# Token-order loads and DMA transposes for q and k of the last batch

## The chip, the cores and the metric

The kernel runs on one core of a Trainium2 chip. The metric is the device time of one execution in microseconds (us), the median of several. The spans in the profiles are about 2 us shorter than the timed executions, because they run from the first to the last instruction. Each execution is listed with the mean granted clock of PE. PE is TensorE's matmuls, DVE VectorE, ACT ScalarE, POOL GpSimd, SP the engine whose queue issues most plain DMAs and all DMA transposes here.

## The reference, cut to what matters

Four batches of attention (8 heads, 768 positions, head size 64; each position sees 8 global and the 96 latest positions), then a mixing block over tokens and channels.

```python
scores = scale * np.matmul(q, k.transpose(0, 1, 3, 2))      # per batch and head
...                                                         # bias by distance, mask
a = np.exp(scores - scores.max(-1)); a = a / a.sum(-1)
x = np.matmul(a, v)                                         # heads side by side: 768 x 512

theta = x @ w_theta
zr, zi = x * np.cos(theta), x * np.sin(theta)
u = x + w_tok_r @ zr + w_tok_i @ zi                         # mixing over tokens, per batch
out = u + np.maximum(u @ w_ch, 0.0)
```

q, k and v are float32; the kernel casts them to bfloat16 while it loads them.

## The kernel before

PE needs q and k with the head dimension on the partitions: `qT` and `kT`, 128 x 768 for a pair of heads. The kernel before loads q and k so that a partition gets six successive tokens of a head (768 B written per row), casts the layout on DVE (`qkn`), transposes 128 x 128 blocks on PE into PSUM and copies them out, qT by DVE and kT by ACT. I call this the prep of a pair. `kG` is a copy of kT in which each block starts with the global positions.

```python
def load_qk(b, h0, n, which=(0, 1)):
    qk = loads[b][0]
    for i_ in which:
        nc.gpsimd.dma_start(
            out=qk[:, i_, h0:h0 + n].rearrange("p h t d -> p h (t d)"),
            in_=(q, k)[i_][b, h0:h0 + n].rearrange("h (p t) d -> p h (t d)", p=T))

def prep(b, p):
    ...                                                     # prep_copy: two DVE casts into qkn
    for i_, dst in ((0, qT), (1, kT)):
        ps = ps_small([T, NT, T], BF)
        with behind("pe"):
            for t_ in range(NT):
                nc.tensor.transpose(ps[:, t_, :], qkn[:, t_, i_].rearrange("p h d -> p (h d)"), ident)
        ...
        if i_ == 0:
            nc.vector.tensor_copy(out=dst, in_=src)
        else:
            nc.scalar.copy(out=dst, in_=src)
    qkT[(b, p)] = [qT, kT, None]
    kglob(b, p)                                             # two DVE copies: kG
```

The main loop runs over the batches. While batch b is mixed (`mix`, `chan`: long matmuls), the attention of batch b + 1 is woven into it by weights (`weave`; its last argument says at which part of the mixing the attention ends). The prep of batch b + 2 is woven in there too (`ahead`). So batch 3, the last, is prepared in the mixing of batch 1. Then comes theta of batch b + 1, which needs `xT`, the transpose of the attention's result; for batches 1 to 3 it is made by DMA, as `uT` is, the transpose of the mixing's result.

```python
def xtrans(b, p, copy=nc.vector.tensor_copy):
    if b:
        nc.sync.dma_start_transpose(
            out=xT_sb[b][:, p, :].rearrange("p (t s) -> p t s", t=NT),
            in_=x_sb[b][:, p].rearrange("p t d -> p (t d)"))
        return
...
ahead = [lambda p=p: prep(b + 2, p) for p in range(NP)] if b + 2 < B else []
order = th[:4] + rest[:2] + th[4:] + rest[2:] if b else []  # theta of b, last chan of b - 1
if b == 1:
    order.insert(0, lambda: load_behind(3, xT_sb[1][0:1, NC - 1, 0:1]))   # q, k, v of batch 3
...
weave(main, side, 0.3 if b == 0 else 0.0, 0.9)
```

A compile-time scheduler settles the order of each engine's and each queue's instructions; every queue then works in that order. `behind(e)` forces an instruction behind the last one that was marked as anchor `e`.

I call the time from the first theta matmul of one batch to that of the next a stage: stage 0 ends with theta of batch 1; stage 1 is theta and mixing of batch 1 with the attention of batch 2, and so on. A "boundary" is the stretch from the first theta matmul to the first score matmul of the next batch.

The softmax here doesn't subtract the row's maximum and nothing guards it: scores larger than these inputs give would overflow.

Of the kernel before, what the change touches and what calls it, by code (L numbers as in the profile page):

```python
# [10 lines left out]
BF = mybir.dt.bfloat16  # L11
# [5 lines left out]
def kernel(  # L17
# [13 lines left out]
    nc = tc.nc  # L31
    B, H, S, D = q.shape
    T = 128
    NT = S // T
    DM = H * D
    NC = DM // T
    NP = H // 2
    NG = int(n_global)
# [9 lines left out]
    att = ctx.enter_context(tc.tile_pool(name="att", bufs=2))  # L48
# [7 lines left out]
    def ps_small(shape, dtype):  # L56
        return small.tile(shape, dtype, name="ps", tag="ps")
# [3 lines left out]
    loads = {}  # L61

    def alloc_qk(b):
        loads[b] = [ld.tile([T, 2, H, NT, D], BF, name="qk"), None]

    def alloc_v(b):
        vn = loads[b][1] = ld.tile([T, H, NT, D + 1], BF, name="vn")
        nc.vector.memset(vn[:, :, :, D:D + 1], 1.0)  # L68
# [4 lines that stand above are left out]
            nc.gpsimd.dma_start(  # L73
                out=qk[:, i_, h0:h0 + n].rearrange("p h t d -> p h (t d)"),
                in_=(q, k)[i_][b, h0:h0 + n].rearrange("h (p t) d -> p h (t d)", p=T))

    def load_v(b, h0, n):
        vn = loads[b][1]
        nc.gpsimd.dma_start(out=vn[:, h0:h0 + n, :, 0:D].rearrange("p h t d -> p (h t) d"),  # L79
                            in_=v[b, h0:h0 + n].rearrange("h (t p) d -> p (h t) d", p=T))  # L80
# [8 lines left out]
    for i_, eng in ((1, nc.sync), (0, nc.scalar)):  # L89
        eng.dma_start(out=qk32[:, i_].rearrange("p h t d -> p h (t d)"),  # L90
                      in_=(q, k)[i_][0, 0:2].rearrange("h (p t) d -> p h (t d)", p=T))
# [5 lines left out]
    alloc_qk(0)  # L97
    alloc_v(0)
    load_qk(0, 2, 2)
    load_v(0, 0, 4)  # L100
    load_qk(0, 4, 2)
    load_qk(0, 6, 2)
    load_v(0, 4, 4)

# [64 lines left out]
    x_sb, xT_sb = {}, {}  # L169
    qkT = {}  # L170

    anchor = {}
# [5 lines left out]
    def behind(eng):  # L178

        return tc.issue_after(anchor[eng]) if eng in anchor else nullcontext()  # L180
# [24 lines left out]
    def kglob(b, p):  # L205
        kT = qkT[(b, p)][1]
        kG = qkT[(b, p)][2] = att.tile([T, NT - 2, T], BF, name="kG", bufs=6)
        nc.vector.tensor_copy(out=kG, in_=kT[:, T:(NT - 1) * T].rearrange("p (t n) -> p t n", t=NT - 2))  # L208
        nc.vector.tensor_copy(out=kG[:, :, 0:NG], in_=kT[:, None, 0:NG].to_broadcast([T, NT - 2, NG]))  # L209

    qkns = {}

    def prep_copy(b, p):
        qk = loads[b][0]
        qkn = qkns[b, p] = att.tile([T, NT, 2, 2, D], BF, name="qkn", bufs=2)
        with behind("dve"):
            for i_ in range(2):
                nc.vector.tensor_copy(  # L218
                    out=qkn[:, :, i_].rearrange("p t h d -> p h t d"), in_=qk[:, i_, 2 * p:2 * p + 2])

    def prep(b, p):
        if p == 0:
            prep_copy(b, 0)
        if p + 1 < NP:
            prep_copy(b, p + 1)
        qkn = qkns[b, p]
        qT = att.tile([T, S], BF, name="qT", bufs=6)
        kT = att.tile([T, S], BF, name="kT", bufs=6)
# [6 lines that stand above are left out]
            dst = dst.rearrange("p (n t) -> p n t", t=NT)  # L235
            src = ps.rearrange("p t n -> p n t")
# [4 lines that stand above are left out]

        qkT[(b, p)] = [qT, kT, None]
        kglob(b, p)

    ebuf = {}

# [51 lines left out]
    def scores(b, p, c):  # L298
        score_mms(b, p, c)
        score_exp(b, p, c)  # L300
# [41 lines left out]

    def xtrans(b, p, copy=nc.vector.tensor_copy):
        if b:
            nc.sync.dma_start_transpose(
                out=xT_sb[b][:, p, :].rearrange("p (t s) -> p t s", t=NT),
                in_=x_sb[b][:, p].rearrange("p t d -> p (t d)"))
            return
        ps = ps_small([T, S], BF)
        for st in range(NT):  # L350
            nc.tensor.transpose(ps[:, st * T:(st + 1) * T], x_sb[b][:, p, st, :], ident)
        copy(out=xT_sb[b][:, p, :], in_=ps)
# [44 lines left out]
    def utrans(b, tt):  # L397
        u = u_sb[b, tt]
        uT = moe.tile([T, NC, T], BF, name="uT", bufs=5)
        uTs[(b, tt)] = uT  # L400
        if b and (b, tt) != (B - 1, NT - 1):
            nc.sync.dma_start_transpose(out=uT, in_=u)
            return
        ps = ps_small([T, NC, T], BF)
        for dc in range(NC):
            nc.tensor.transpose(ps[:, dc, :], u[:, dc * T:(dc + 1) * T], ident)  # L406
        nc.scalar.copy(out=uT, in_=ps)  # L407
# [16 lines left out]
    def load_all_qk(b):  # L424
        alloc_qk(b)
        load_qk(b, 0, 8)

    def load_all_v(b):
        alloc_v(b)
        load_v(b, 0, 8)  # L430
# [4 lines left out]
    def load_behind(b, tile):  # L435
        g = nc.gpsimd.tensor_copy(out=gate, in_=tile).ins
        with tc.issue_after(g):
            load_all_qk(b)
            load_all_v(b)

    def attention_steps(b, preps):

        steps = []
        add = lambda w, f, *a: steps.append((w, lambda: f(*a)))
        add(0, alloc_x, b)
        chunks = [(p, c) for p in range(NP) for c in range(NT // 2)]
        ahead = [preps[:1], preps[1:2], preps[2:]] if preps else [[]] * 3
        for i_ in range(0, len(chunks), 2):
            steps.append((1800, lambda i_=i_: [scores(b, *pc) for pc in chunks[i_:i_ + 2]]))
            if i_ == 0:  # L450
                add(0, vglob, b, 0, H)
            if i_ == 8:
                steps.extend((1536, f) for f in ahead[0])
            for p in [p for p in range(NP) if (i_ // 2, p) in ((2, 0), (3, 1), (5, 2))]:
                add(1600, lambda p=p: [values(b, p, 0), values(b, p, 1)])
                add(800, xtrans, b, p)
        steps.extend((1536, f) for f in ahead[1])
        add(1600, lambda: [values(b, NP - 1, 0), values(b, NP - 1, 1)])
        add(800, xtrans, b, NP - 1)
        steps.extend((1536, f) for f in ahead[2])  # L460
        return steps
# [22 lines left out]
    dve, act = nc.vector.tensor_copy, nc.scalar.copy  # L484
# [24 lines left out]
    for p in range(NP):  # L509
# [29 lines left out]
        if p:  # L539
            xtrans(0, p - 1, act if p == NP - 1 else dve)  # L540
# [14 lines left out]
    for b in range(B):  # L555
        nxt = b + 1 if b + 1 < B else None
        lag = 3
        th = [lambda c=c, j=j: theta(b, c, j) for c in range(NT // 2) for j in range(2)]
        pre = [lambda p=p: prep(1, p) for p in range(NP)] if b == 0 else []
        ahead = [lambda p=p: prep(b + 2, p) for p in range(NP)] if b + 2 < B else []  # L560
        order = th[:4] + rest[:2] + th[4:] + rest[2:] if b else []
        if b == 1:
            order.insert(0, lambda: load_behind(3, xT_sb[1][0:1, NC - 1, 0:1]))
        for f in order:
            f()
        main = []
        for tt in range(NT):
            for g in range(NT // 2):
                if (b, tt) != (B - 1, NT - 1):
                    main.append((2048, lambda tt=tt, g=g: mix(b, tt, g)))  # L570
                if b == 0 and g == 1 and tt + 1 < NT:
                    main.append((1536, lambda tt=tt: trans_w(tt + 1)))
                if tt >= lag and g == 0 and (b, tt) != (B - 1, NT - 1):
                    main.append((2048, lambda tt=tt: chan(b, tt - lag)))
                if b == 0 and tt and g == 1:
                    main.append((512, lambda tt=tt: utrans(b, tt - 1)))
            if b and (b, tt) != (B - 1, NT - 1):
                main.append((0, lambda tt=tt: utrans(b, tt)))
        side = [(1536, f) for f in pre]
        if b == 0:  # L580
            side[:0] = [(0, lambda: load_all_v(2))]
        side += attention_steps(nxt, ahead) if nxt else []
        weave(main, side, 0.3 if b == 0 else 0.0, 0.9)
        rest = [lambda tt=tt, b=b: chan(b, tt) for tt in range(NT - lag, NT)]
        if b == 0:
            rest.insert(1, lambda b=b: utrans(b, NT - 1))
# [44 lines left out]
```

## Time and profile before

The time was 176.44 us, the median of three (176.27 to 177.23). The profiled execution has a span of 174.7 us at clock 1.000.

The first parts of the page give busy time and share of the span, then the busy tenths in 40 slices of 4.4 us (9 is 90% or more; DMA is the mean of 16 DMA engines).

```profile
PE 160.6 (92%) x1505; PEld 86.4 (49%) x1530; DVE 133.9 (77%) x300; ACT 102.2 (58%) x128; POOL 26.3 (15%) x31
...
DVE  7678965778999999996779999796866847723443
...
DMA  5999999999999972479999955133145371414335
```

PE is nearly always busy. DVE is full from slice 11 to 18 (stage 0) and again from slice 22 to 25 (the end of stage 1). The DMA engines are full until about 60 us, and once more around 80 to 100 us, when batch 3 is loaded.

The prep's groups (line, engine, operation, out<-in, shape, count, then total busy us and mean ns of one, then the idle time before them). Each group is for three batches; a third is batch 3's.

```profile
L238 DVE COPY qT<-ps 128x768 bf16<-128x768 bf16 x12 | 11.4, 947 | 0.0
L233 PE MATMUL ps<-ident,qkn 128*128 128x128 bf16 x144 | 10.7, 219 | 0.4 <-DVE qkn L218 0.3
L240 ACT COPY kT<-ps 128x768 bf16<-128x768 bf16 x12 | 9.6, 798 | 10.3 <-PE ps L233 10.3
L218 DVE COPY qkn<-qk 128x768 bf16<-128x768 bf16 x24 | 7.4, 342 | 0.0
```

The busy time overlaps for pipelined instructions. What a prep costs PE is read better from the chain that ended last (start, length, what), where batch 3's four preps stand:

```profile
94.93 0.67 PE ps L233 x12
...
100.46 0.67 PE ps L233 x12
...
104.39 0.67 PE ps L233 x12
...
105.95 0.87 PE ps L233 x12
```

Busy time by stretches (start:end, length, then PE, PEld (weight loads), DVE, ACT and POOL, then granted clock, DMA share and GB/s) for stage 1 and for stage 2, which has the same mixing and attention but no prep:

```profile
72.00:108.50 36.50, 35.79 (x347) 19.46 (x351) 32.68 (x72) 24.59 (x30) 4.77 (x4) 1.00 1.26 156
108.50:142.00 33.50, 32.91 (x294) 16.58 (x298) 25.23 (x47) 19.63 (x23) 0.00 (x0) 1.00 0.34 84
```

PE (the first engine) binds in both; stage 1 is 3 us longer. The theta lines of PE's timeline, with the idle time before them in brackets:

```profile
108.38 3.62 PE L368 MATMUL pb<-w_theta_bf,xT 128*128 128x512 bf16 x15
...
141.48 1.46 PE L368 MATMUL pb<-w_theta_bf,xT 128*128 128x512 bf16 x6
143.44 2.33 PE L368 MATMUL pb<-w_theta_bf,xT 128*128 128x512 bf16 x10 [0.50 <-DMA xT<-x_sb]
```

Theta of batch 2 (108.38) runs through.

### The profile page before, as it was taken

What the parts mean: (1) busy time and instruction counts of PE and PEld (TensorE: products, weight loads), DVE (VectorE), ACT (ScalarE), POOL (GpSimd) and SP (SyncE); (2) the same over time, 40 slices, a digit from 0 to 9 for tenths busy, and PEclk for the clock granted to TensorE, in tenths of its full rate; (3) what the DMA queues carried; (4) which work ended last, traced back from release to release, by engine and by line L of the source; (5) the groups of instructions that cost most, each with busy time, mean ns of one, the idle gap of its engine ahead of it and who ended that gap; (6) DMA issues with size and microseconds to landing.
All of it is one profiled execution on the core that took longest, in us unless ns stands there. A gap on an engine that the chain in (4) does not pass through costs nothing.

```text
span 174.7 us, 3707 instructions
## 1 busy us (share of the span) xinstructions
PE 160.6 (92%) x1505; PEld 86.4 (49%) x1530; DVE 133.9 (77%) x300; ACT 102.2 (58%) x128; POOL 26.3 (15%) x31
## 2 busy tenths in 40 slices
PE   6469878999999899999999999999999989999991
PEld 1245555456746566544455565443554634444440
DVE  7678965778999999996779999796866847723443
ACT  2479676999497694499854813779447408500010
POOL 8983355004000000190000000000000000000000
PEclk9999999999999999999999999999999999999999
DMA  5999999999999972479999955133145371414335
GB/s 157 183 192 182 206 208 208 204 205 165 166 204 167 159 116 45 109 90 216 244 148 103 168 135 135 34 121 90 21 87 134 90 168 27 172 31 101 114 90 180
DMA packets 58225, 24.36 MB, mean 139 GB/s; under 512 B 44256, under 2 KB 55264, under 8 KB 58208
## 3 DMA queue, kind: packets, MB, share of 16 engines
q0 software_dynamic: 35216, 12.45, 70.5%
q1 hardware_dynamic: 22576, 11.15, 28.8%
q10 hardware_dynamic: 416, 0.52, 0.9%
q8 instruction: 12, 0.20, 0.5%
q14 instruction: 5, 0.04, 0.1%
HBM read 25.69 MB, written 6.29 MB: 183 GB/s over the span
## 4 chain that ended last, share of the span: by engine, by line
PE 56%; DVE 23%; ACT 13%; DMA 4%; issue 2%; DVEq 0%; ACTq 0%
PE ps L388 25%; PE ps L413 10%; PE pb L368 7%; DVE x_sb L341 4%; PE pb L274 4%; PE pb L331 3%; ACT e L281 3%; PE ps L368 3%; ACT etab L133 3%; ACT cs L374 3%; DVE qT L238 2%; DVE e L291 2%; DMA qk<-in_k_dram 2%; DVE kG L208 2%; PE ps L233 2%
## 5 line engine op out<-in xcount | busy, mean ns | idle before, releaser
L388 PE MATMUL ps<-zri,w_tokT 128*128 128x512 bf16 x271 | 67.6, 379 | 1.2 <-issue 0.5
L281 ACT ACTIVATE e<-pb 128x1024 bf16<-128x1024 f32 (+1 forms) x48 | 43.5, 958 | 21.1 <-PE pb L274 21.0
L388 PEld LDWEIGHTS <-w_tokT 128*128 128x128 bf16 x288 | 25.9, 98 | 27.6 <-DVE w_tokT L160 0.6
L393 DVE TENSOR_TENSOR u<-x_sb,ps 128x512 bf16<-128x512 bf16 x24 | 16.4, 682 | 14.0 <-PE ps L388 14.0
L413 PE MATMUL ps<-w_ch_bf,uT 128*128 128x512 bf16 x94 | 23.7, 379 | 0.3 <-DVE u L393 0.2
L377 DVE TENSOR_TENSOR zri<-x_sb,cs 128x512 bf16<-128x512 bf16 x48 | 17.9, 418 | 7.9 <-ACT cs L374 7.6
L419 DVE SCALAR_TENSOR_TENSOR o_sb<-ps,u 128x512 f32<-128x512 f32 (+1 forms) x25 | 16.5, 662 | 3.1 <-PE ps L413 3.1
L274 PE MATMUL pb<-qT,kT 64*128 64x128 bf16 x224 | 15.6, 219 | 1.4 <-DVE qT L202 0.3
L291 DVE TENSOR_TENSOR e<-e,etab 128x1024 bf16<-128x1024 bf16 (+1 forms) x24 | 14.7, 616 | 2.5 <-ACT e L281 2.5
L274 PEld LDWEIGHTS <-kT 64*128 64x128 bf16 x224 | 9.1, 94 | 14.5 <-issue 12.5
L374 ACT ACTIVATE cs<-pb,halfpi 128x1024 bf16<-128x1024 f32 x8 | 8.9, 1115 | 11.5 <-PE pb L368 11.5
L240 ACT COPY kT<-ps 128x768 bf16<-128x768 bf16 x12 | 9.6, 798 | 10.3 <-PE ps L233 10.3
L368 PE MATMUL pb<-w_theta_bf,xT 128*128 128x512 bf16 x62 | 14.9, 379 | 0.6 <-DMA xT<-x_sb 0.5
L407 ACT COPY uT<-ps 128x512 bf16<-128x512 bf16 x7 | 4.1, 587 | 18.6 <-PE ps L406 18.6
L368 PEld LDWEIGHTS <-xT 128*128 128x128 bf16 x96 | 9.2, 98 | 11.1 <-DMA xT<-x_sb 1.0
L331 PEld LDWEIGHTS <-e 128*128 128x128 bf16 x352 | 12.6, 97 | 3.3 <-issue 1.6
L413 PEld LDWEIGHTS <-uT 128*128 128x128 bf16 x96 | 8.9, 98 | 10.0 <-ACT uT L407 0.3
L274 PE MATMUL pb<-qT,kG 64*128 64x128 bf16 x128 | 11.7, 217 | 1.5 <-DVE kG L209 1.4
L341 DVE TENSOR_TENSOR x_sb<-pb,rec 128x768 bf16<-128x768 f32 x12 | 11.4, 948 | 0.2
L79 POOL DMA_DIRECT2D vn<-in_v_dram x5 | 9.6, 1912 | 12.2 <-DVE vn L68 10.6
L238 DVE COPY qT<-ps 128x768 bf16<-128x768 bf16 x12 | 11.4, 947 | 0.0
L233 PEld LDWEIGHTS <-qkn 128*128 128x128 bf16 x144 | 9.0, 97 | 4.4 <-DVE qkn L218 1.4
(72 smaller groups left out, 200.9 us busy)
## 6 DMA issues: line engine op xcount, KB each, us to landing
out_dram<-o_sb SPq DMA_DIRECT2D x23, 256.0 KB, 2.2
qk<-in_q_dram POOLq DMA_DIRECT2D x3, 768.0 KB, 17.4
qk<-in_k_dram POOLq DMA_DIRECT2D x3, 768.0 KB, 19.3
vn<-in_v_dram POOLq DMA_DIRECT2D x3, 768.0 KB, 22.0
w_nat<-in_moe_w_tok_r_dram POOLq DMA_DIRECT2D x3, 384.0 KB, 14.0
w_nat<-in_moe_w_tok_i_dram POOLq DMA_DIRECT2D x3, 384.0 KB, 15.2
vn<-in_v_dram POOLq DMA_DIRECT2D x2, 384.0 KB, 8.8
qk<-in_q_dram POOLq DMA_DIRECT2D x3, 192.0 KB, 6.7
```

The lines of the kernel that those rows point to most:

```text
L238: nc.vector.tensor_copy(out=dst, in_=src)
L274: nc.tensor.matmul(pb[:, hh, o:o + T], lhsT=lhsT, rhs=qT[R, (own, nxt)[part]], start=bool(b), stop=bool(b) or (jt == NT - 1 or (j == 1 and ...
L281: ins = nc.scalar.activation(e_c, pb[:, :, 0:n], AF.Exp, scale=scale).ins
L291: nc.vector.tensor_mul(e_c, e_c, tab[:, :, s0:s0 + n // T].rearrange("p a s n -> p a (s n)"))
L331: nc.tensor.matmul(o, lhsT=l_, rhs=r_, start=(i_ == 0), stop=(i_ == len(mms) - 1))
L341: nc.vector.tensor_mul(xv, po4[:, :, :, 0:D], rec.to_broadcast([T, n, NT, D]))
L368: nc.tensor.matmul(pb[j_] if last else pb[:, j_, :], lhsT=xT[:, dc, st(j_)], rhs=w_theta_bf[:, dc, :], start=(dc == 0), stop=(dc == NC - 1))
L377: nc.vector.tensor_mul(zri[b][:, i_, 2 * c + j_, :].rearrange("p (g d) -> p g d", g=NP), xb[:, :, 2 * c + j_, :], cs[:, i_, j_].rearrange( ...
L388: anchor["pe"] = nc.tensor.matmul(ps, lhsT=w_tokT[wi][:, st, tt * T:(tt + 1) * T], rhs=zri[b][:, wi, st, :], start=(st == 0 and wi == 0), ...
L393: anchor["dve"] = nc.vector.tensor_add(u_sb[b, tt].rearrange("p (g d) -> p g d", g=NP), x_sb[b][:, :, tt, :], ps.rearrange("p (g d) -> p g ...
L413: nc.tensor.matmul(ps_c, lhsT=uT[:, dc, :], rhs=w_ch_bf[:, dc, :], start=(dc == 0), stop=(dc == NC - 1))
L419: nc.vector.scalar_tensor_tensor(o_sb[:, cols], in0=ps_c[:, cols], scalar=0.0, in1=u[:, cols], op0=ALU.max, op1=ALU.add)
```

## The change

Its intent: take the prep of the last batch off PE, DVE and ACT. q and k of batch 3 are loaded in token order (a partition is a token within a block of 128, both heads of a pair side by side), so that one DMA transpose makes a whole qT or kT. The first four heads are loaded in stage 0, behind the last casts of batch 1, the others at the start of stage 1. Pair 0 is transposed in the mixing of batch 1, pairs 1 to 3 at the boundary to batch 2. The kG copies are made when the attention of batch 3 begins.

```diff
--- before.py
+++ after.py
@@ -74,6 +74,15 @@
                 out=qk[:, i_, h0:h0 + n].rearrange("p h t d -> p h (t d)"),
                 in_=(q, k)[i_][b, h0:h0 + n].rearrange("h (p t) d -> p h (t d)", p=T))
 
+    def load_qk_tokens(b, h0, n):
+        qk = loads[b][0]
+        for h in range(h0, h0 + n):
+            for i_ in range(2):
+                pair = qk[:, i_, h // 2 * 2:h // 2 * 2 + 2].rearrange("p h t d -> p (h t d)")
+                nc.gpsimd.dma_start(
+                    out=pair.rearrange("p (t h d) -> p t h d", t=NT, h=2)[:, :, h % 2],
+                    in_=(q, k)[i_][b, h].rearrange("(t p) d -> p t d", p=T))
+
     def load_v(b, h0, n):
         vn = loads[b][1]
         nc.gpsimd.dma_start(out=vn[:, h0:h0 + n, :, 0:D].rearrange("p h t d -> p (h t) d"),
@@ -205,8 +214,10 @@
     def kglob(b, p):
         kT = qkT[(b, p)][1]
         kG = qkT[(b, p)][2] = att.tile([T, NT - 2, T], BF, name="kG", bufs=6)
-        nc.vector.tensor_copy(out=kG, in_=kT[:, T:(NT - 1) * T].rearrange("p (t n) -> p t n", t=NT - 2))
-        nc.vector.tensor_copy(out=kG[:, :, 0:NG], in_=kT[:, None, 0:NG].to_broadcast([T, NT - 2, NG]))
+        with behind("dve") if b == B - 1 else nullcontext():
+            nc.vector.tensor_copy(
+                out=kG, in_=kT[:, T:(NT - 1) * T].rearrange("p (t n) -> p t n", t=NT - 2))
+            nc.vector.tensor_copy(out=kG[:, :, 0:NG], in_=kT[:, None, 0:NG].to_broadcast([T, NT - 2, NG]))
 
     qkns = {}
 
@@ -241,6 +252,16 @@
 
         qkT[(b, p)] = [qT, kT, None]
         kglob(b, p)
+
+    def prep_dma(b, p):
+        qk = loads[b][0]
+        qkT[(b, p)] = [None, None, None]
+        for i_ in (1, 0):
+            to = qkT[(b, p)][i_] = att.tile([T, S], BF, name=("qT", "kT")[i_], bufs=6)
+            with behind("sp"):
+                nc.sync.dma_start_transpose(
+                    out=to.rearrange("p (t s) -> p t s", t=NT),
+                    in_=qk[:, i_, 2 * p:2 * p + 2].rearrange("p h t d -> p (h t d)"))
 
     ebuf = {}
 
@@ -342,9 +363,9 @@
 
     def xtrans(b, p, copy=nc.vector.tensor_copy):
         if b:
-            nc.sync.dma_start_transpose(
+            anchor["sp"] = nc.sync.dma_start_transpose(
                 out=xT_sb[b][:, p, :].rearrange("p (t s) -> p t s", t=NT),
-                in_=x_sb[b][:, p].rearrange("p t d -> p (t d)"))
+                in_=x_sb[b][:, p].rearrange("p t d -> p (t d)")).ins
             return
         ps = ps_small([T, S], BF)
         for st in range(NT):
@@ -399,7 +420,7 @@
         uT = moe.tile([T, NC, T], BF, name="uT", bufs=5)
         uTs[(b, tt)] = uT
         if b and (b, tt) != (B - 1, NT - 1):
-            nc.sync.dma_start_transpose(out=uT, in_=u)
+            anchor["sp"] = nc.sync.dma_start_transpose(out=uT, in_=u).ins
             return
         ps = ps_small([T, NC, T], BF)
         for dc in range(NC):
@@ -435,7 +456,7 @@
     def load_behind(b, tile):
         g = nc.gpsimd.tensor_copy(out=gate, in_=tile).ins
         with tc.issue_after(g):
-            load_all_qk(b)
+            load_qk_tokens(b, H // 2, H // 2)
             load_all_v(b)
 
     def attention_steps(b, preps):
@@ -445,10 +466,14 @@
         add(0, alloc_x, b)
         chunks = [(p, c) for p in range(NP) for c in range(NT // 2)]
         ahead = [preps[:1], preps[1:2], preps[2:]] if preps else [[]] * 3
+        if b == B - 1:
+            add(0, kglob, b, 0)
         for i_ in range(0, len(chunks), 2):
             steps.append((1800, lambda i_=i_: [scores(b, *pc) for pc in chunks[i_:i_ + 2]]))
             if i_ == 0:
                 add(0, vglob, b, 0, H)
+            if b == B - 1 and i_ in (0, 2, 6):
+                add(0, kglob, b, (1, 2, 0, 3)[i_ // 2])
             if i_ == 8:
                 steps.extend((1536, f) for f in ahead[0])
             for p in [p for p in range(NP) if (i_ // 2, p) in ((2, 0), (3, 1), (5, 2))]:
@@ -557,8 +582,11 @@
         lag = 3
         th = [lambda c=c, j=j: theta(b, c, j) for c in range(NT // 2) for j in range(2)]
         pre = [lambda p=p: prep(1, p) for p in range(NP)] if b == 0 else []
-        ahead = [lambda p=p: prep(b + 2, p) for p in range(NP)] if b + 2 < B else []
+        ahead = [[lambda p=p: prep(2, p) for p in range(NP)], [lambda p=p: prep_dma(3, p) for p in range(1)],
+                 [], []][b]
         order = th[:4] + rest[:2] + th[4:] + rest[2:] if b else []
+        if b == 2:
+            order[:0] = [lambda p=p: prep_dma(3, p) for p in range(1, NP)]
         if b == 1:
             order.insert(0, lambda: load_behind(3, xT_sb[1][0:1, NC - 1, 0:1]))
         for f in order:
@@ -579,6 +607,7 @@
         side = [(1536, f) for f in pre]
         if b == 0:
             side[:0] = [(0, lambda: load_all_v(2))]
+            side.append((0, lambda: (alloc_qk(3), load_qk_tokens(3, 0, H // 2))))
         side += attention_steps(nxt, ahead) if nxt else []
         weave(main, side, 0.3 if b == 0 else 0.0, 0.9)
         rest = [lambda tt=tt, b=b: chan(b, tt) for tt in range(NT - lag, NT)]
```

## The prediction

> **What bounds the kernel.** The page gives PE 160.6 of 174.7 us (92%), DVE 77%, ACT 58%. In the mixing of batch 0 (about 42 to 69 us) DVE is busy 4.0 of every 4 us and the chain of waits runs on DVE; from 69 us on the chain is almost all PE. Theta of batches 1, 2 and 3 starts at 71.9, 108.4 and 141.5 us (timeline of PE). Stage 1 (mixing of batch 1 beside the attention of batch 2) lasts 36.5 us with PE busy 35.8 (busy time by stretches); stage 2, the same work without a prep of q and k, lasts 33.1 us plus a 0.5 us wait of theta for the DMA of xT.
>
> **What goes.** Batch 3's prep, all in stage 1: 48 PE transposes in four groups of 12, 0.67 us each on the chain (at 94.9, 100.5, 104.4, 106.0 us), 2.7 us; on DVE 8 casts of 0.28 and 4 qT copies of 0.87 us (5.7 us); on ACT 4 kT copies of 0.80 us. DVE is 98% busy from 96.0 to 108.5, but over the stage PE binds, so only PE's 2.7 us count.
>
> **What comes or moves.** Eight DMA transposes of 128x768 on SP, each like those of xT: 1.2 us of the queue, 2.8 us to landing on a quiet DMA. Two sit in stage 1; six (7.3 us of SP's queue) follow the last uT of batch 1 at 109.3 us. They delay three output stores (four buffers, next user over 8 us later) and land before pair 1 is needed at about 120 us: no cost. Batch 3's kG copies (4 x about 0.3 us) move to stage 2, where DVE is busy 25 of 33.5 us: no cost.
>
> The token-order loads have 64-element rows, 128 B written, like v. The Trainium skill ("DMA: Bandwidth & Descriptors", Specifications) puts line rate at 512 B or more. Yet here v of batch 3 lands 7.9 us after k, and k 6.4 us after q, of the same bytes: small rows cost 1 to 2 us of DMA, off the path. What matters is when: the first half is now queued at about 46 to 52 us, behind v of batch 2 (landing 61.3), so the DMA engines stay full until about 69.5. The same page ("Issuing engines are not separate DMA queues") says that all queues interleave on the same engines; the trace agrees: a transpose of xT took 6.7 us under load against 2.8. Those of batch 1 at 60 and 66 us will take 6 to 7; the last (issued about 70.5, landing 73.0) should just escape. I allow 0.3 us.
>
> **On the path.** Minus 2.7 us of PE. Given back: without the prep transposes at 104 to 107 us, which filled PE while the last xT of batch 2 was in flight, theta of batch 2 should wait for that DMA as theta of batch 3 does, about 0.5 us. 176.4 - 2.7 + 0.5 + 0.3 = about 174.5 us, 1.1% less.
>
> **What will show it.** Prep transposes fall from 144 to 96; theta to theta of stage 1 from 36.5 to about 34 us; a wait of PE for the DMA of xT near 105 us; the other stages unchanged to 0.4 us; xT near 60 to 70 us landing in up to 7 us.
>
> **What would make it wrong.** The early load reaching beyond 71 us and holding the last xT of batch 1, so that theta stalls by 2 to 4 us; the scheduler ordering other work anew; SP's queue holding a uT or xT behind the added transposes; a kG copy of batch 3 holding DVE at the boundary. Better than thought: DVE's relief closing PE gaps (0.7 us in stage 1).

## More of the kernel before

Theta of batch 3 stops after six matmuls and waits for the last DMA transpose of x. The end of a matmul is modelled, so the stop is better read from the starts: the six and the ten matmuls start 1.96 us apart, and six take 1.30 us at the pace of the others (0.216 us each). The stop is 0.66 us.

## The result

The changed kernel took 174.65 us (median of 4, 174.29 to 174.73), the one before 176.59 us in all its runs so far. A ratio here is the mean time of one kernel's runs over that of the other's of the same rounds, so it is not quite the ratio of the medians. It was 0.9882, with a 95% interval of 0.9849 to 0.9914: 1.2% faster. When I ran it again in later rounds (e0 below), it was 0.9933 (0.9904 to 0.9963). Executions over 1.5% slower than the fastest of the same kernel are left out of the means.

In the page after, PE's load and DVE's fell (PE's by only 0.7 us, at least in part because the trace before lacks some matmuls: x271 of the mixing's on its page, x288 after), and the DMA engines are now full up to slice 16:

```profile
PE 159.9 (93%) x1482; PEld 83.5 (48%) x1482; DVE 128.5 (74%) x288; ACT 99.1 (57%) x124; POOL 37.9 (22%) x45
...
DVE  7678965678999999999587588597786837724443
...
DMA  5999999999999999879999997787138571323335
```

The prep groups have lost the third that was batch 3's (144 to 96 transposes on PE):

```profile
L249 DVE COPY qT<-ps 128x768 bf16<-128x768 bf16 x8 | 7.5, 942 | 0.0
L244 PE MATMUL ps<-ident,qkn 128*128 128x128 bf16 x96 | 7.3, 219 | 0.6 <-DVE qkn L229 0.3
L251 ACT COPY kT<-ps 128x768 bf16<-128x768 bf16 x8 | 6.4, 798 | 4.9 <-PE ps L244 4.9
L229 DVE COPY qkn<-qk 128x768 bf16<-128x768 bf16 x16 | 5.0, 338 | 0.0
```

PE's timeline after: theta of batch 1, then the boundary to batch 2, then theta of batch 3.

```profile
72.19 0.59 PE L389 MATMUL pb<-w_theta_bf,xT 128*128 128x512 bf16 x2
...
105.40 1.46 PE L389 MATMUL pb<-w_theta_bf,xT 128*128 128x512 bf16 x6
107.39 2.33 PE L389 MATMUL pb<-w_theta_bf,xT 128*128 128x512 bf16 x10 [0.53 <-DMA xT<-x_sb]
...
114.27 1.02 PE L409 MATMUL ps<-zri,w_tokT 128*128 128x512 bf16 x4 [0.23 <-DVE o_sb L440]
...
139.41 1.46 PE L389 MATMUL pb<-w_theta_bf,xT 128*128 128x512 bf16 x6
141.34 2.33 PE L389 MATMUL pb<-w_theta_bf,xT 128*128 128x512 bf16 x10 [0.47 <-DMA xT<-x_sb]
```

Theta of batch 2 now starts at 105.40 instead of 108.38, but it stops as batch 3's does, and there is a second stop before the mixing at 114.27. The table splits both spans at these marks (each number is a difference of two starts in PE's timeline, or to the end of the span).

| us | before | after | difference |
|---|---|---|---|
| start to theta of batch 1 | 71.87 | 72.19 | +0.32 |
| stage 1: theta of batch 1 to theta of batch 2 | 36.51 | 33.21 | -3.30 |
| boundary: theta of batch 2 to first scores of batch 3 | 8.73 | 9.82 | +1.09 |
| first scores to theta of batch 3 | 24.37 | 24.19 | -0.18 |
| theta of batch 3 to the end | 33.2 | 33.2 | 0.0 |
| span | 174.7 | 172.6 | -2.1 |

The 1.09 us of the boundary are two stops. The first is theta's for xT: from 105.40 to 107.39 are 1.99 us for six matmuls that take 1.30, so 0.7 us. The second is read in the same way: four chan matmuls start at 113.01 and take 0.87 us, the mixing starts at 114.27, so 0.4 us. It waits for DVE's `o_sb` (in brackets), which reads a chan product out of PSUM and so frees a buffer that the mixing writes. DVE's timeline shows why that came late:

```profile
109.18 0.76 DVE L398 TENSOR_TENSOR zri<-x_sb,cs 128x512 bf16<-128x512 bf16 x2 [1.34 <-ACT cs L395]
110.63 0.30 DVE L218 COPY kG<-kT 128x512 bf16<-128x512 bf16 x1 [0.69 <-DMA kT<-qk]
110.84 0.75 DVE L398 TENSOR_TENSOR zri<-x_sb,cs 128x512 bf16<-128x512 bf16 x2
```

The scheduler put a kG copy of pair 1 of batch 3 between zri products of batch 2, and DVE, which works in order, stood for 0.69 us until the DMA transpose of kT had landed; the zri products and the `o_sb` behind the copy came later by as much.

The added transposes in SP's queue (start, how long SP was held, what):

```profile
96.81 1.26 SPq L262 DMA_TRANSPOSE kT<-qk  x1
98.17 1.28 SPq L262 DMA_TRANSPOSE qT<-qk  x1
...
101.93 1.25 SPq L366 DMA_TRANSPOSE xT<-x_sb  x1
103.28 1.21 SPq L423 DMA_TRANSPOSE uT<-u  x1
104.58 1.24 SPq L366 DMA_TRANSPOSE xT<-x_sb  x1
```

Each holds SP for 1.2 to 1.3 us. The last xT of batch 2 is issued at 104.58 and lands 2.8 us later, just when theta goes on. DVE had completed its x at 104.24 us (a start of 103.28 and 0.96 us), so the uT ahead of it in SP's queue held it up by 0.3 us. Most of the stop has another reason, which e2b shows.

### The profile page after: what moved, and what is told of

It is laid out like the page before. It is cut to its first block, busy times and chain, and to the rows that moved or that the text cites. A ratio compares the mean times of both kernels' runs of the same rounds, so it can differ in the third digit from the quotient of the medians.

```text
span 172.6 us, 3652 instructions
## 1 busy us (share of the span) xinstructions
PE 159.9 (93%) x1482; PEld 83.5 (48%) x1482; DVE 128.5 (74%) x288; ACT 99.1 (57%) x124; POOL 37.9 (22%) x45
## 3 DMA queue, kind: packets, MB, share of 16 engines
q0 software_dynamic: 45680, 12.45, 78.4%
## 4 chain that ended last, share of the span: by engine, by line
PE 59%; DVE 21%; ACT 10%; DMA 6%; issue 1%; SPq 0%; DVEq 0%; ACTq 0%
PE ps L409 29%; PE ps L434 10%; PE pb L389 5%; PE pb L295 4%; PE pb L352 4%; DVE x_sb L362 4%; ACT etab L142 3%; PE ps L389 3%; ACT e L302 3%; DMA qk<-in_k_dram 3%; DVE kG L218 2%; DVE e L312 2%; ACT cs L395 2%; DMA kT<-qk 2%; DMA xT<-x_sb 2%; PE ps L244 2%
## 5 line engine op out<-in xcount | busy, mean ns | idle before, releaser
L409 PE MATMUL ps<-zri,w_tokT 128*128 128x512 bf16 x288 | 70.6, 380 | 0.3 <-DVE o_sb L440 0.2
L434 PE MATMUL ps<-w_ch_bf,uT 128*128 128x512 bf16 x96 | 24.2, 379 | 0.0
L315 DVE TENSOR_TENSOR e<-e,etab 128x1024 bf16<-128x1024 bf16 x12 | 8.2, 684 | 2.8 <-ACT e L302 2.8
L352 PE MATMUL pb<-vn,e 128*128 128x65 bf16 x168 | 9.6, 193 | 0.3 <-DVE x_sb L362 0.3
L82 POOL DMA_DIRECT2D qk<-in_q_dram x8 | 7.4, 920 | 8.8 <-DVE qkn L229 5.0
```

What stands on the lines that cost most here:

```text
L352: nc.tensor.matmul(o, lhsT=l_, rhs=r_, start=(i_ == 0), stop=(i_ == len(mms) - 1))
L409: anchor["pe"] = nc.tensor.matmul(ps, lhsT=w_tokT[wi][:, st, tt * T:(tt + 1) * T], rhs=zri[b][:, wi, st, :], start=(st == 0 and wi == 0), ...
L434: nc.tensor.matmul(ps_c, lhsT=uT[:, dc, :], rhs=w_ch_bf[:, dc, :], start=(dc == 0), stop=(dc == NC - 1))
```

## The experiments

My theory: the gain is PE's time for the 48 transposes in stage 1, and it is partly given back where a transpose of x, now without preps to hide behind, is waited for, and where the kG copy waits. Rivals: DVE's relief (5.7 us, and DVE was 98% busy at the end of stage 1), or a better order of the loads. Twelve kernels ran. Those that only add unused work give the right result; all outputs were correct. Stage lengths are from the one profiled execution of each.

### e0: the changed kernel again

> The changed kernel again, in the same rounds as the three that follow, as their yardstick. Both theories: 174.6 us, 0.988 of before.

175.04 us (174.56 to 176.53), 0.9933 of before. Its profile has the same boundary (9.79 us), but stage 1 is 34.25 us instead of 33.21. Two waits appear which the first profile did not have: theta of batch 1 for its xT (0.21 us), and the first chan of batch 1 for its uT, which took 9.5 us to land (84.4 to 93.9 us) while the end of the second half and then v were loading:

```profile
93.95 1.04 PE L434 MATMUL ps<-w_ch_bf,uT 128*128 128x512 bf16 x4 [0.55 <-DMA uT<-u]
```

So the waits for transposes beside the loads differ between these two profiles by 0.8 us; the change works close to an edge here.

### e1: PE's work put back

```diff
+    def fake_pe(p):
+        for i_ in range(2):
+            ps = ps_small([T, NT, T], BF)
+            with behind("pe"):
+                for t_ in range(NT):
+                    nc.tensor.transpose(ps[:, t_, :], w_theta_bf[:, t_ % NC, p * T:(p + 1) * T], ident)
-    [lambda p=p: prep_dma(3, p) for p in range(1)],
+    [lambda: (prep_dma(3, 0), fake_pe(0))] + [lambda p=p: fake_pe(p) for p in range(1, NP)],
```

> The changed kernel with 48 PE transposes of a weight tile put back at the places of the old preps (results unused, no copy out of PSUM, output stays right). Theory PE (the gain is PE's 2.7 us in stage 1): plus 2.7 us of work, minus most of the 0.5 us wait for the last xT, which they fill again: 176.7 us, stage 1 from 33.2 back to about 36 us. Rival DVE (the gain is the 5.7 us taken from a DVE that was 98% busy at the end of stage 1) and rival DMA (the gain is that batch 3's second half and v land sooner, so that uT and xT of stage 1 land sooner): within 0.4 us of the changed kernel, 174.6 us.

177.59 us, 1.0070 of before (1.0052 to 1.0088). Stage 1 is 36.29 us, 3.08 us more than in the first profile of the changed kernel, and 2.80 us more than in e0 with e0's two waits (0.76 us) taken off. So 48 transposes cost PE about 2.8 to 3.1 us, 58 to 64 ns each, and with them the whole gain is gone. The wait for xT is gone, as predicted (but e1 restores more than the transposes there, see e2b). What I had not expected is that the boundary stayed at 9.59 us: DVE's wait for kT grew to 1.2 us. Counted from the start of theta, kT landed about as before, but theta no longer stopped, so DVE came to the kG copy sooner. Presumably the stop for xT had been hiding part of the stop for kG; no run tests that alone.

### e2 and e2b: DVE's work put back

```diff
+    def fake_dve(p):
+        qk = loads[3][0]
+        with behind("dve"):
+            for i_ in range(2):
+                cast = att.tile([T, NT, 2, 2, D], BF, name="qkn", bufs=2)
+                nc.vector.tensor_copy(out=cast[:, :, i_].rearrange("p t h d -> p h t d"), in_=qk[:, i_, 0:2])
+            slow = att.tile([T, S], BF, name="slow", bufs=1)
+            ...                      # e2: a strided bf16 add; e2b: a float32 add of 768 columns
```

> The changed kernel with DVE work like that of the old preps put back at their places: 8 copies of 128x768 and 4 slow strided adds of 128x768 into unused tiles, about 5.5 us in all, no PE work. Theory PE: at most 0.4 us slower, 174.6 to 175.0 us. Rival DVE: nearly the whole gain is lost, about 176.3 us. Rival DMA: 174.6 us.

e2 took 178.31 us, 1.0101 of before, which looked like the rival's victory. But the profile shows that the dose was wrong: each strided add took 1.75 us on the chain, so DVE got 9.3 us back and not 5.7. Stage 1 was 33.61 us nevertheless; the loss came at the boundary (12.83 us), where theta stopped for xT (0.7 us), and then PE stopped twice for DVE's `o_sb` (1.3 and 0.9 us, about 1 us of work between them) and its granted clock then halved, at 116.9 us. So I repeated it.

> The DVE test again with a smaller dose: in the earlier one each slow add took 1.75 us instead of 0.87, 9.3 us in all. Now the adds read float32 without stride, some 0.87 us each, 5.7 us in all, as in the old preps. Theory PE (48 PE transposes were worth about 3.1 us of stage 1, DVE 0.2): stage 1 stays within 0.4 us of 33.2 us, and the total within 0.8 us of the changed kernel, because DVE enters the boundary to batch 2 a little behind. Rival DVE: the total goes back to that of before or above, 176.4 us or more.

With the adds at 0.87 us on the chain (5.7 us in all, the last 1.4 us of it after theta had begun), stage 1 is 33.61 us again and the total 174.03 us, 0.9853 of before (0.9834 to 0.9871). The rival falls: of stage 1's 3 us, DVE's work is worth at most 0.4 us (33.61 against 33.21), and kernels without it came as high (e8, 33.60). The boundary was 8.73 us, exactly that of the kernel before, with neither stop. PE's timeline shows where the first of them went. First the changed kernel, from the end of the last value products to theta (which starts at 105.40), then e2b:

```profile
102.81 1.03 PE L434 MATMUL ps<-w_ch_bf,uT 128*128 128x512 bf16 x4
103.67 1.89 PE L409 MATMUL ps<-zri,w_tokT 128*128 128x512 bf16 x8
...
101.51 1.89 PE L420 MATMUL ps<-zri,w_tokT 128*128 128x512 bf16 x8
103.24 1.03 PE L445 MATMUL ps<-w_ch_bf,uT 128*128 128x512 bf16 x4
104.10 1.89 PE L420 MATMUL ps<-zri,w_tokT 128*128 128x512 bf16 x7
105.83 3.62 PE L400 MATMUL pb<-w_theta_bf,xT 128*128 128x512 bf16 x16
```

In e2b theta starts 4.3 us after the last value products, in the changed kernel 2.6 us: eight mixing matmuls (1.7 us) more stand in between (one record is missing from the x7). `weave` spaces its steps by their weights. In the kernel before, two prep steps stood behind the last value products; with them gone these moved two groups, eight matmuls, towards the end of the mixing. e1, e2, e2b and e3 have four steps in the places of the preps, and with them the old order of PE. (Run by hand with these weights, `weave` gives 16 mixing matmuls behind the last value products for the kernel before and these four, and 8 for the changed kernel, as the traces show.) On SP's queue the last xT is also ahead of a uT (the line left out is an output store):

```profile
101.58 1.24 SPq L377 DMA_TRANSPOSE xT<-x_sb  x1
...
103.53 1.26 SPq L377 DMA_TRANSPOSE xT<-x_sb  x1
104.89 1.21 SPq L434 DMA_TRANSPOSE uT<-u  x1
```

It was issued 1 us sooner than in the changed kernel, 0.1 us after its x was complete (103.41 us), and theta did not stop. The scheduler also put the kG copy of pair 1 behind the zri products. So a kernel with useless work has the lowest median of all, by the luck of an order. The same weave with empty steps in place of the useless work was not tried.

### e3: the loads alone, transposed on PE

```diff
+    def prep_tok(b, p):
+        ...
+            flat = qk[:, i_, 2 * p:2 * p + 2].rearrange("p h t d -> p (h t d)")
+            for t_ in range(NT):
+                nc.tensor.transpose(ps[:, t_, :], flat[:, t_ * T:(t_ + 1) * T], ident)
+            (nc.scalar.copy if i_ else nc.vector.tensor_copy)(out=to, in_=ps.rearrange("p t n -> p (t n)"))
-    [lambda p=p: prep_dma(3, p) for p in range(1)],
+    [lambda p=p: prep_tok(3, p) for p in range(NP)],
-    if b == 2: order[:0] = [lambda p=p: prep_dma(3, p) for p in range(1, NP)]
```

> Token-order loads in two halves as in the change, but batch 3 is transposed on PE in stage 1 at the old places, straight from the loaded tile: no casts, and a contiguous copy out of PSUM. PE work of stage 1 is that of before; DVE gets about 4 x 0.55 us back out of 5.7; no added DMA transposes. Theory PE: stage 1 near 36 us, no wait for the last xT, 176.5 us, so like before. Rival DVE: most of the gain stays, about 175.2 us. Rival DMA: all of it stays, 174.6 us.

176.48 us, 1.0015 of before (0.9999 to 1.0031); stage 1 36.29 us, boundary 8.73 us. (The kG copies are back at their old places too, an edit cut from the diff.) The token-order loads with their early half gain nothing by themselves, although the casts are gone and the copies of qT fell from 0.95 to 0.55 us each. Together with e1 this is the verdict on both rivals: with PE's transposes in stage 1 there is no gain, whatever DVE and the loads do. ACT's four kT copies (0.80 us each) were not put back alone; in e1 they are gone as well, and the gain with them is not there, so their relief is worth nothing by itself.

### e4: the whole load at the start of stage 1

```diff
-            side.append((0, lambda: (alloc_qk(3), load_qk_tokens(3, 0, H // 2))))
...
-            load_qk_tokens(b, H // 2, H // 2)
+            alloc_qk(b)
+            load_qk_tokens(b, 0, H)
```

> The changed kernel with all of batch 3's q and k, still in token order, loaded at the start of stage 1 (no early half). Theory (the early half delays transposes of xT in stage 0 and costs 0.3 us there): theta of batch 1 starts 0.3 us earlier, xT of batch 1 lands within 7 us again, uT and xT of stage 1 land later (load until about 97 us) at no cost: 0.2 to 0.4 us faster than the changed kernel. Rival (the halves are needed: loading late delays the first DMA transposes and stage 1's uT): slower by 0.5 us or more.

179.87 us, 1.0188 of before (1.0160 to 1.0216); my expectation was wrong and the rival right. Theta of batch 1 did start earlier (71.59 us), but stage 1's DMA transposes now ran beside the load. SP was held for 2.1 to 2.3 us by three of them in a row (97.66 to 104.40 us), the last two xT of batch 2 were issued at 105.12 and 107.76, and theta stood for 2.9 us. The boundary took 15.18 us, because the clock fell as well (see e5). So the early half in stage 0 is not a detail: it pays some tenths there to keep SP and the DMA engines free at the end of stage 1.

### e5: two pairs in the mixing, two at the boundary

```diff
-    [lambda p=p: prep_dma(3, p) for p in range(1)],
+    [lambda p=p: prep_dma(3, p) for p in range(2)],
-            order[:0] = [lambda p=p: prep_dma(3, p) for p in range(1, NP)]
+            order[:0] = [lambda p=p: prep_dma(3, p) for p in range(2, NP)]
```

> The changed kernel with pairs 0 and 1 transposed in the mixing of batch 1 and pairs 2 and 3 at the boundary. Theory: at the boundary a kG copy of pair 1 stood before the zri products on DVE and waited for the DMA of kT, which PE felt as 0.4 us; this wait goes, 0.4 us faster than the changed kernel, and the wait of kG for kT is no longer in the list of waits. Rival (that wait is hidden behind the wait for xT): no change, within 0.1 us.

1.0119 of before (1.0077 to 1.0160; two of its six runs counted as slow and are left out, which makes it look better than it is, see below). The kG copies no longer wait, as expected, but something worse came:

```profile
102.83 1.25 SPq L366 DMA_TRANSPOSE xT<-x_sb  x1
104.18 1.23 SPq L262 DMA_TRANSPOSE kT<-qk  x1
105.51 1.23 SPq L262 DMA_TRANSPOSE qT<-qk  x1
106.84 1.21 SPq L423 DMA_TRANSPOSE uT<-u  x1
108.15 1.24 SPq L366 DMA_TRANSPOSE xT<-x_sb  x1
```

The second pair stands between the last two xT. DVE had finished x of the last pair at 105.28 us (a start of 104.32 and 0.96 us), but SP issued its transpose at 108.15, 2.9 us late. PE waited, and then ran slowly:

```profile
110.99 3.71 PE L389 MATMUL pb<-w_theta_bf,xT 128*128 128x512 bf16 x10 [3.09 <-DMA xT<-x_sb]
```

```profile
110.00:111.00 1.00, 0.01 (x1) 0.02 (x2) 0.00 (x0) 0.00 (x0) 0.00 (x0) 0.71 0.83 221
111.00:112.00 1.00, 1.00 (x3) 0.41 (x4) 0.00 (x0) 0.00 (x0) 0.00 (x0) 0.50 0.96 236
```

The third number from the end is the granted clock: it halved during the wait and stayed at 0.50 until about 113.8 us. The ten matmuls of theta took 3.55 us from start to start instead of 2.17. The Trainium skill ("TensorE: Matmul & The Clock Gate", Part 1: The HAM clock gate) tells of this: a PE idle for about one window of 3.4 us drops to half its clock; here it fell 2.5 us after PE had gone idle (see the closing list). So a wait of 3.1 us made a boundary that is 4.6 us longer than in the kernel before (13.37 against 8.73). The mean clock of e5's six runs goes with their time: 1.0 and 0.996 in the two fastest (177.75 and 178.11 us), 0.979 to 0.990 in the other four, two of which (180.66 and 180.93 us) are those labelled slow. All six runs of e4 had 0.977 to 0.990, while the kernel before, on the same chip in the same rounds, had 0.997 to 1.000. So the lower clock belongs to the kernels with the long stop, not to the chip's state, and in e5 it comes in some runs only.

### e6 and e10: one mend each

e6 weaves the attention of batches 2 and 3 to end earlier; e10 forces the kG copy of pair 1 behind the zri products.

```diff
-        weave(main, side, 0.3 if b == 0 else 0.0, 0.9)
+        weave(main, side, 0.3 if b == 0 else 0.0, 0.9 if b == 0 else 0.85)      # e6
...
...                                                          # e10 also makes the zri products an anchor
-        with behind("dve") if b == B - 1 else nullcontext():                     # kglob
+        with behind("zri" if p == 1 else "dve") if b == B - 1 else nullcontext(): # e10
```

> The changed kernel with the attention of batches 2 and 3 woven to end at 0.85 of the mixing instead of 0.9, which puts four matmuls of mixing (0.86 us) between the last value products and the theta that needs their transpose. Theory: both waits of theta for xT (0.7 and 0.65 us, read as the break in the run of matmuls) vanish, but at the boundary to batch 2 PE then waits so much longer for the zri products that stand behind the kG copy: net 0.7 us faster than the changed kernel. Rival (kG's wait is no limit): 1.3 us faster.

> The changed kernel with one order forced: on DVE the kG copy of pair 1 of batch 3 comes after the zri products of batch 2, not before. Theory (in the changed kernel DVE stood still behind that copy until kT had landed, and PE felt it as 0.4 us at the boundary): from the first theta matmul of batch 2 to the first score matmul of batch 3 9.4 us instead of 9.8, total 0.4 us less than the changed kernel. Rival (hidden behind ACT's sines, which pace zri anyway): no change, within 0.1 us in the boundary.

e6: 174.62 us, 0.9905 of before. Theta of batch 3 does not stop any more (theta to end 32.57 instead of 33.2 us). At the boundary 0.34 us of listed wait for xT remain: SP issued the last xT at 104.70, right behind a uT, 0.9 us after its x was complete (103.79). The first uT of batch 1 was waited for as well (0.38 us in stage 1, which took 33.84 us). e10: 174.60 us, 0.9893 of before. The kG stop is gone: the chan matmuls at 113.14 are followed by the mixing at 114.00 without a gap. Yet the boundary shrank only to 9.62 us, since the wait for xT was 0.2 us longer in that run. Neither total differs from the changed kernel's by more than its own scatter, so the gains that either theory expected (0.4 to 1.3 us) did not come.

### e8: two pairs together, earlier, and a tighter weave

```diff
+    [lambda: (prep_dma(3, 0), prep_dma(3, 1))],
+            order[:0] = [lambda p=p: prep_dma(3, p) for p in range(2, NP)]
+        weave(main, side, 0.3 if b == 0 else 0.0, 0.9 if b == 0 else 0.8)
```

> Meant to beat both: pairs 0 and 1 transposed together at the earlier place in the mixing of batch 1 (four DMA transposes on SP before xT of pair 2, not between xT of pair 2 and xT of pair 3 as in the run with two in the mixing), and the attention of batches 2 and 3 woven to end at 0.8 of the mixing. Theory (the give-back is the wait for the last xT, 0.7 us at the boundary to batch 2 and 0.6 at that to batch 3, and kG's wait for kT, 0.4 us): all three go, about 1.7 us less than the changed kernel, 172.9 us; theta of batch 2 to first scores 8.8 us. Rival (four transposes in the mixing always hold up the last xT): PE waits for xT by 1 us or more at the boundary to batch 2, and the total is no better than the changed kernel.

176.41 us, 1.0007 of before: all of the gain is lost, as the rival said. Four transposes in a row filled SP from 96.44 to 102.95 us, the third xT of batch 2 went out at 104.35 instead of 101.93, and theta stopped twice (0.83 and 0.90 us). The tighter weave cost another 0.9 us: from the first scores to theta of batch 3 it took 25.1 us instead of 24.2, with PE's score matmuls waiting for ACT (0.4 us are listed). Here PE's order was no remedy: 16 mixing matmuls stood before theta, but the last xT was issued 3.4 us after its x was complete (102.86 us), behind the added transposes.

### e7c: batch 2 instead of batch 3

```diff
-    load_all_qk(2)
+    alloc_qk(2)
+    load_qk_tokens(2, 0, H)
...
+    [lambda: prep_dma(2, 0), lambda: None] + [lambda p=p: prep_dma(2, p) for p in range(1, NP)],
+    [lambda p=p: prep(3, p) for p in range(NP)],            # batch 3 as in the kernel before
```

> The same idea for batch 2 instead of batch 3 (batch 3 as in the kernel before): q and k of batch 2 in token order in their old place in the load queue, one pair transposed by DMA in the mixing of batch 0 and three behind the last xT of batch 1; kG copies of pairs 1 to 3 behind the zri products. Theory of the stages (stage 0 is bound by DVE and nearly by PE, so there both the 5.7 us of DVE and the 3.1 us of PE count): theta of batch 1 about 3 us earlier than 71.9 us, total about 173.5 us. Rival (stage 0 is where the DMA engines are full and where xT of batch 1 needs them): theta of batch 1 waits 3 us or more for its last xT, the clock falls to half behind that wait, and the total is 177 us or more.

184.85 us, 1.0445 of before: the rival by far. Stage 0 would have had more to gain, but it is where the DMA engines are full. The first kT took 10.9 us to land, xT 9.7 us, theta of batch 1 stood for 4.75 us, and the clock was halved behind it, and again at 93.9 us (mean of the run 0.970). It differs from the changed kernel in more than one thing (which batch and stage; and the kG copies of pairs 1 to 3 stand behind the zri products here, an edit cut from the diff), so it shows that this placement loses, and where, but it does not isolate the load of the DMA engines as the cause.

### e11: both mends

e6 and e10 in one kernel.

> The two mends that each took away a wait, together, meant to beat both kernels: kG of pair 1 behind the zri products, and the attention of batches 2 and 3 woven to end at 0.85 of the mixing; one pair in the mixing as in the change. Theory: theta of batch 2 to first scores 9.1 us instead of 9.8 (kG's 0.4 us gone, the wait for xT about 0.3 us smaller, since SP issues it right behind a uT), no break in theta of batch 3 (0.6 us), total about 173.3 us, 1.3 us less than the changed kernel, 0.983 of before. Rival (what is taken away comes back at the next wait, as in the two runs with one mend each): 174.3 us or more.

174.46 us, 0.9881 of before (0.9859 to 0.9904): the best of my mends, steadier than the changed kernel (174.12 to 174.58), but not clearly faster than its first measurement (0.9882), and 1.2 us over what I expected. The boundary fell to 9.27 us and theta of batch 3 ran through (32.55 us to the end). But the first uT was again waited for (0.40 us in stage 1), and the tighter weave gave 0.68 us back between the first scores and theta of batch 3 (24.87 instead of 24.19), where the list of waits now has 0.6 us of PE waiting for ACT's `e`. A wait taken away came back at the next place. I found no deliberate version that beats the changed kernel by a clear margin; the accidental one (e2b) differs in the order of PE, of SP and of DVE. In e11 itself theta still stopped for 0.5 us: 12 mixing matmuls stand behind the last value products, and the last xT was issued 0.9 us after its x was complete (103.99 us), behind a uT. A kernel with it forced ahead of that uT is left untried.

## Why the prediction was right

The time was forecast as 174.5 us and measured as 174.65 (175.04 in e0); 1.1% less was forecast, and the ratio says 1.2% (0.7% in e0). Point by point:

- **PE bounds stage 1, and only PE's part counts.** Right. e1 (PE back, gain gone), e2b (DVE back, gain kept) and e3 (PE transposes with the new loads, no gain) show it. The size was put at 2.7 us and was 2.8 to 3.1. Stage 1 as a whole lost 3.3 us in the first profile, and 2.9 to 3.1 in e2b, e8 and e10 (33.44 to 33.61 us). That DVE's part counts for nothing is shown to within 0.4 us.
- **Theta of batch 2 will wait for xT like batch 3's, about 0.5 us.** Right in kind: 0.53 us is listed, 0.7 us by the starts. It came at 107.4 us, where I had said near 105. The reason given (the prep transposes that had filled PE are gone) is only part of it. Between the last value products and theta the kernel before has 24 of them (1.3 us) and 16 mixing matmuls, the changed kernel no transposes and 8 mixing matmuls (1.7 us less). e2b has no transposes but 16 mixing matmuls, and does not stop. So the forecast was right partly by luck: the moved order of PE was not foreseen.
- **A kG copy holding DVE at the boundary** stood among what could go wrong, not in the sum ("no cost"). It did happen: 0.69 us on DVE, 0.4 us on PE. This term was missed. e10 took it away.
- **The early load costs 0.3 us in stage 0.** The first profile shows 0.32 us, but over the eleven profiles with the early half theta of batch 1 starts anywhere from 71.75 to 72.55 us, so one number proves little. What the load did is in the next point.
- **"Small rows cost 1 to 2 us of DMA, off the path."** Too small. The first half took 8.9 us (v of batch 2 landed at 61.8 us, the last k of the half at 70.7), where k of batch 2, the same bytes in long rows, had landed 3.9 us after its q in the kernel before, though without DMA transposes beside it. The second half took 12.8 us from its first issue to its last landing (73.8 to 86.6 us), where q of batch 3 in long rows took 8.1 us. So batch 3's v landed at 95.2 us, hardly earlier than the 96.1 of the kernel before, though half of q and k were there already. The profile's pages agree: the same 12.45 MB of that queue went from 35216 packets and 70.5% of the engines' span to 45680 packets and 78.4%. The Trainium skill's 512 B for line rate ("DMA: Bandwidth & Descriptors", Specifications) fits this better than my reading of one v load. It was nearly free in the first profile; in e0 waits of 0.76 us stood beside it.
- **Eight DMA transposes on SP at no cost.** Right for this placement, but for kG's wait above, and not for the others tried. e5 and e8 show how little room there is: with two more transposes before the last xT, e5 (median 179.67 us) was 5 us slower than the changed kernel, and e8 (with a tighter weave as well) lost the whole gain.
- **The other stages unchanged.** Within 0.2 us.

The sum came out right partly because misses cancelled: 3.3 instead of 2.7 in stage 1, and 1.1 instead of 0.5 given back at the boundary. That the number is off by only 0.15 us is luck; that PE's transposes are the gain is not.

## What to carry to other kernels

Here, taking work off the engine that binds a stage was worth that engine's share of it (2.8 to 3.1 us), and DVE's 5.7 us were worth at most 0.4; test it by putting each part back alone, and check the dose. A DMA transpose is not free: here it held its queue for 1.2 us, and the transfers that the critical engine waits for must not stand behind it, so place it by the order of that queue and by how full the DMA engines are. When a step disappears from a woven schedule, look at which latency it was hiding and at where the steps beside it move. And remember that here waits of 2.9 to 4.8 us on PE (e4, e7c, and e5 in its profiled run) also halved the clock behind them.

## What the Trainium skill lacked or had wrong

- "DMA: Bandwidth & Descriptors" (DMA Transpose): it does not say how long a queue is held by a transpose from SBUF to SBUF of this size on trn2 (cycle counts of earlier generations stand only beside those of trn3, for other sizes). Here a transpose of 128 x 768 bfloat16 held SP for 1.2 us, and successive ones started 1.33 us apart. That is 196,608 B in 1.33 us or 148 GB/s, below the 261 GB/s that the page gives as effective bandwidth ("Latency and other measured facts", measured on one other kernel). Under load SP was held for up to 2.7 us (e4), in e7c once for 5.2 us.
- The same page says that issuing from several engines only saves the sequencer's time ("Issuing engines are not separate DMA queues"). The sharing of the DMA engines agrees with the runs (xT landing after 8.7 us under load against 2.7). It calls that time usually small; for these transposes it was 1.2 of 2.8 us to landing. What it lacks is that the order within one issuing queue can decide: one transpose issued 2.9 us late on SP made e5's boundary 4.6 us longer than one without a stop.
- "TensorE: Matmul & The Clock Gate" (Part 1: The HAM clock gate) speaks of one idle window of about 3.4 us until the clock halves, and of gaps over about 3 us ("Why this matters for your kernels"). Here less was enough. In e4 it fell at about 107.6 us and in e5 at about 110.4 us (from the clock records of the traces), 2.3 and 2.5 us after PE had gone idle. In e2 it fell at 116.9 us, 3.2 us after the first of two stops had begun, although PE had worked for 1 us in between. In each of these traces the changes of the clock stand whole multiples of 3.413 us apart, so the window before a drop can be placed: PE was busy in it for 1.1 us (e4), 0.9 us (e5) and 1.3 us (e2). That a window with some work in it counts as idle, the page doesn't say. In e7c the first drop, at 73.4 us, came after a window of no work at all, as the page says, the second, at 93.9 us, after one with 1.7 us.
- "DMA: Bandwidth & Descriptors" ("Why small descriptors are slow") puts the overhead of a 256-byte descriptor at 27%. Here half of q and k (1.57 MB of float32, read in rows of 256 B and written in rows of 128 B) took 8.9 us in stage 0, where the same bytes in long rows had landed in 3.9 us, and 12.8 us in stage 1, where they had taken 8.1 us. Part of this may be the cast, the load by others (DMA transposes of x ran beside the half in stage 0), or eight issues in place of one, which no run separates.
